# Zero warm-up, fewer first masks, a last fold in two parts and re-placed sums and loads in a fused attention, Fourier-mix and FFN kernel

## The chip, the cores and the metric

The kernel runs on 1 core of one Trainium2 chip. The metric is device time in microseconds (us) of one execution; lower is better. The engines are TensorE (PE, with its weight loads shown apart as PEld), VectorE (DVE), ScalarE (ACT), GpSimd (POOL) and SyncE (SP), which here issues nearly all DMAs.

## The reference

Windowed attention with sink tokens, then a block that adds a real 2-D Fourier transform, normalises, and runs a two-layer FFN. Shapes: 4 batches, 8 heads, 768 tokens, head size 64; so 512 channels, and a hidden size of 2048. All in float32; `n_sink` is 4 and `window` is 128.

```
scores = q @ k.T / sqrt(D)
keep   = (key < n_sink) | (0 <= query - key < window)
a      = softmax(where(keep, scores, -1e9))            # + 1e-9 in the denominator
x      = (a @ v), heads side by side                   # [4, 768, 512]
u      = x + real(fft(fft(x, tokens), channels))
un     = (u - mean(u)) / sqrt(var(u) + 1e-6)           # per token
out    = u + relu(un @ w_ch1) @ w_ch2                  # w_ch1 [512, 2048], w_ch2 [2048, 512], float64
```

## The kernel before

**Tiling.** Tokens are handled in 24 blocks of 128 (6 per batch, batches in the order 0, 2, 1, 3). One step of the attention loop (`window_attention`, L719) handles one pair of heads of one block, so 4 steps per block, 96 in all, numbered s. Every engine has an order of operations written out by hand for each of the four steps (`SCHEDULE`, L83), with delays against the step at which the scores were made (`STEP_LAG`, `BLOCK_AT`). Work beside the attention is hung into those steps by `at(step, engine, function)` and run by `run_ev`.

**The first steps.** The masks depend on `n_sink` and `window`, which a small DMA brings (`prm`, L242). VectorE builds mask 0 before step 0, all other masks but the last in `other_masks` (L971) in step 1, and `last_mask` (L985) in step 3. `mask[i]` is used by block i of a batch (block 3 and later use `mask[3]`), and `older[0]`, `older[1]` choose in `merge` (L788) between two key blocks. In step 3 also the sink values of batch 0 are split into a high and a low half (`SINK0_AT`, L763 to L769). TensorE meanwhile runs transposes of the identity that nobody reads (`warm_up`, L958): 11 before step 0 and 8, 0, 8, 4, 8, 4, 0 in steps 0 to 6.

**The Fourier part** of a batch (`fourier`, L336) begins when its blocks are there: `fold_n` (sums and differences of two token blocks), `fold_m` (the same along the channels), `fold_hi` and `fold_lo` (a float32r high half `gh` by ScalarE and a low half `gl` by VectorE), `stage1` (matmuls along the tokens; kinds a0, a1, r, b0, b1 by channel range), `stage2a/b` (along the channels), `combine` and `update` (add to the token block `u`). For the last batch (`tail`) the three folds all run on VectorE. Up to step 97 the program order is the order on each engine; from there to group 1 of the FFN a scheduler orders the instructions by readiness, with the program order as priority. `tc.issue_after(x)` holds an instruction behind x in that ordering.

**The FFN** works on 6 groups of 4 token blocks. Group 0 (the loop at L1343) goes through the 16 blocks f of the hidden size: `ch1` (12 matmuls of 512 columns, L703), `split` (relu and its high half on ScalarE, low half on VectorE, L1191), and one block behind it `ch2` (12 matmuls, L1199). In the same loop the float64 weights are turned into float32 pairs (`convert`, L627: three integer operations on VectorE, a copy on ScalarE, a subtraction on GpSimd: L651 for the first layer, L666 for the second). `combine_w1` (L671) forms sums of weight blocks on GpSimd (`tq`, four operations of 128x256, then two of 128x512 in `halves`, L686) and stores them to DRAM (`w_dram`), because groups 1 to 5 use a seven-product scheme (Strassen's, in Winograd's form) whose weights are such sums. Group 1's token side (`prepare_1`, L1261: statistics, normalising, transposing, then seven steps of token sums `sums_x`, L1284) also lies in this loop, three steps per block from f = 6 on.

**Group 1** (from L1405, again in hand-written order) streams its weight sums back: `load(n)` (L1390) issues two DMAs of 256 KB on SP into place n modulo 8; seven of the eight places are filled before group 1 starts, after all stores of `w_dram`. `product` (L1414) does 12 matmuls of 256 columns and issues the load for eight products later. `hring` (four slots, in the memory of `un_slots`, that is of `unT0`, which `ch1` of group 0 reads) takes the hidden values of group 1. `todo` (L1503) places group 2's statistics, normalising and transposes among group 1's steps; 10 steps make one of its four rounds `it`. Groups 2 to 5 have the same structure among themselves and are not touched, except by the places that `load` uses.

## Time and profile before

| | us |
|---|---|
| median of 3 runs | 746.86 (746.4 to 748.05) |
| the profiled execution's own time | 747.63 |
| its span (first to last instruction) | 745.9 |
| TensorE busy in the span | 715.6 (96%) |
| VectorE, ScalarE, GpSimd busy | 560.5 (75%), 357.3 (48%), 274.4 (37%) |

The time of the run contains 1.7 us that lie outside the span. Busy times of TensorE contain modelled ends, so a busy TensorE can still be held up a little; an idle one certainly is. The share over the whole span says little about this change, which touches the first 20 us, and the stretch from about 200 to 350 us. There the views by stretch and the lists in order of time have to be read.

### The profile page before, as it was taken

How to read it: one execution, taken by the hardware profiler on the slowest of the kernel's cores; microseconds unless marked ns; L12 is line 12 of the kernel's file. 1: busy time of each engine (PE TensorE's matmuls, PEld its weight loads, DVE VectorE, ACT ScalarE, POOL GpSimd, SP SyncE). 2: the span in 40 equal slices, each digit the busy share in tenths (PEclk: the TensorE clock that was granted, in tenths of full speed). 3: DMA queues.
4: the chain of work that ended last, by engine and by line, in shares of the span. 5: the costliest groups of instructions: out<-in, count | busy, mean ns of one | idle time of the engine just before them, and what ended most of it. 6: DMA issues, size and time to landing. Idle time of an engine off the chain costs nothing.

```text
span 745.9 us, 15695 instructions
## 1 busy us (share of the span) xinstructions
PE 715.6 (96%) x5539; PEld 642.6 (86%) x5539; DVE 560.5 (75%) x1299; ACT 357.3 (48%) x901; POOL 274.4 (37%) x391
## 2 busy tenths in 40 slices
PE   8999998989979999898999999999999999999996
PEld 6776876867868888687989999999999999999996
DVE  7778578888899988858668667947697578846773
ACT  5887666766634537313324134534444245523541
POOL 3567467577557989824994000000000000000000
PEclk9999999999999999999999999999999999999998
DMA  9863525533207999779999798979974897759721
GB/s 304 289 173 106 149 73 165 174 94 103 86 21 237 328 346 330 277 277 385 374 301 327 246 348 277 313 239 379 375 242 167 321 378 261 255 205 390 269 98 62
DMA packets 109576, 181.69 MB, mean 244 GB/s; under 512 B 9868, under 2 KB 44812, under 8 KB 108336
## 3 DMA queue, kind: packets, MB, share of 16 engines
q1 hardware_dynamic: 109200, 176.83, 69.6%
q0 software_dynamic: 288, 3.76, 1.3%
q8 instruction: 46, 0.75, 0.4%
q14 instruction: 42, 0.34, 0.1%
HBM read 148.04 MB, written 32.51 MB: 242 GB/s over the span
## 4 chain that ended last, share of the span: by engine, by line
PE 50%; DVE 4%; ACT 1%; issue 1%; SPq 0%; DMA 0%; POOL 0%; DVEq 0%
PE pB L1421 10%; PE qB L1598 9%; PE pA L1421 7%; PE pC L1421 6%; PE qC L1598 6%; PE qA L1598 6%; PE o L1449 5%; DVE bn L530 1%; PE unt L571 1%; DVE hring L1193 0%; DVE x L1657 0%; DVE x L1660 0%; SPq L1394 0%; DVE un L565 0%; DVE stat L531 0%
## 5 line engine op out<-in xcount | busy, mean ns | idle before, releaser
L1620 ACT CAST hring<-x 128x512 fp32r<-128x512 f32 x92 | 57.0, 619 | 52.0 <-PE qB L1598 19.6
L811 ACT ACTIVATE sm<-sm,mx 128x132 f32<-128x132 f32 x192 | 75.9, 400 | 4.6 <-DVE mx L805 4.6
L1624 DVE TENSOR_TENSOR hring<-x,hring 128x512 fp32r<-128x512 f32 x92 | 63.4, 689 | 14.8 <-ACT hring L1620 9.3
L786 PE MATMUL s<-ring,q 64*128 64x260 f32 x320 | 49.0, 411 | 5.9 <-DVE mx L805 2.7
L805 DVE CUSTOM_DVE_ANT_0 sm<-s,mask 128x132 f32<-128x132 f32 x192 | 48.5, 293 | 6.2 <-DVE s L792 0.9
L703 PE MATMUL h<-un_slots,w_ring 128*128 128x512 f32 x192 | 49.7, 405 | 3.4 <-POOL w_ring L651 2.9
L703 PEld LDWEIGHTS h<-un_slots,w_ring 128*128 128x128 f32 x192 | 36.3, 194 | 12.4 <-POOL w_ring L651 4.1
L786 PEld LDWEIGHTS s<-ring,q 64*128 64x128 f32 x320 | 26.9, 185 | 18.2 <-issue 5.0
L1598 PE MATMUL qA<-w,hring 128*128 128x256 f32 x312 | 39.8, 279 | 0.0
L1449 PE MATMUL o<-w,hring 128*128 128x512 f32 x156 | 38.5, 393 | 1.3 <-ACT hring L1192 1.1
L850 ACT COPY pta<-pt 128x512 f32<-128x512 f32 x48 | 28.1, 585 | 24.1 <-PE pt L843 24.0
L881 PE MATMUL xt<-ptl,ldv 128*64 128x128 f32 x384 | 39.3, 285 | 0.0
L1199 PE MATMUL o<-w,h_sb 128*128 128x512 f32 x156 | 38.1, 392 | 0.0
L1598 PEld LDWEIGHTS qA<-w,hring 128*128 128x128 f32 x312 | 37.9, 189 | 0.0
L811 ACT ACTIVATION_READ_ACCUMULATOR sm<-sm,mx 128x1 f32 x192 | 36.7, 191 | 0.0
L792 DVE COPY_PREDICATED s<-older,s 128x256 f32<-128x256 uint8 x80 | 33.7, 421 | 3.1 <-PE s L786 3.1
L859 POOL TENSOR_SCALAR_AFFINE_SELECT ptl<-pta 128x512 f32<-128x512 f32 x48 | 31.5, 655 | 11.6 <-ACT pta L850 11.6
L1598 PE MATMUL qB<-w_c,hring 128*128 128x256 f32 x288 | 35.2, 281 | 0.0
L1449 PEld LDWEIGHTS o<-w,hring 128*128 128x128 f32 x156 | 28.5, 188 | 7.5 <-ACT hring L1192 1.3
L881 PEld LDWEIGHTS xt<-ptl,ldv 128*64 128x64 f32 x384 | 22.1, 136 | 14.6 <-issue 4.8
L1598 PEld LDWEIGHTS qB<-w_c,hring 128*128 128x128 f32 x288 | 34.5, 189 | 0.0
L1199 PEld LDWEIGHTS o<-w,h_sb 128*128 128x128 f32 x156 | 29.1, 188 | 6.1
(296 smaller groups left out, 1965.3 us busy)
## 6 DMA issues: line engine op xcount, KB each, us to landing
w_c<-wd SPq DMA_DIRECT2D x96, 256.0 KB, 5.0
w_h<-wd SPq DMA_DIRECT2D x76, 256.0 KB, 5.1
w_t<-wd SPq DMA_DIRECT2D x70, 256.0 KB, 4.7
raw<-in_moe_w_ch_dram SPq DMA_DIRECT2D x32, 512.0 KB, 4.5
w_c<-td SPq DMA_DIRECT2D x48, 256.0 KB, 4.6
w_q<-wd SPq DMA_DIRECT2D x38, 256.0 KB, 5.0
wd<-to SPq DMA_DIRECT2D x8, 1024.0 KB, 6.4
ldv<-in_v_dram SPq DMA_DIRECT2D x28, 256.0 KB, 3.3
```

Of the source, the lines that this page charges most:

```text
L703: T.matmul(ps[:, :tb], a[cc], x[:, :, cc, :], start=n == 0, stop=n == 3 * NCC - 1)
L786: T.matmul(ps[:, j, :P + W], st["q", g][rows, hp, :], keys(g, 2 * hp + j), start=True, stop=True)
L792: V.copy_predicated(ps[:, :, P + NS:P + W], older[qi > 2], ps[:, :, 0:P])
L805: V.tensor_tensor_reduce(sm[:, h % 4], ps[:, j, P:P + W], mask[min(qi, 3)], -SCALE, 3.0e38, ALU.add, ALU.min, accum_out=mx[:, 0, h:h + 1])
L811: A.activation(sm[:, h % 4], sm[:, h % 4], AF.Exp, bias=mx[:, 0, h:h + 1], scale=-1.0, accum_out=mx[:, 1, h:h + 1])
L881: T.matmul(ps[D * j:D * j + D, p, :], st["v", kb(g) - i][:, h, :], a[:, h % 4, :], start=i == 0, stop=i == n - 1)
L1199: T.matmul(po[i], a[:, P * i:P * i + P], x, start=f == 0 and n == 0, stop=f == NF - 1 and n == 2)
L1421: T.matmul(ps[:, 256 * j:256 * j + 256], w[:, j, a, cs], x[:, xs], start=BANK.index(BANK[k]) == k and j == c == m == 0, stop=j == c == 1 a ...
L1449: T.matmul(po[i], h[:, a, j, ts_], x, start=first and j == m == 0, stop=last and j == 1 and m == 2)
L1598: T.matmul(ps[:, 256 * t:256 * t + 256], h[:, a, j, P * t:P * t + P], x, start=BANK.index(BANK[k]) == k and c == t == j == m == 0, stop=c ...
L1620: A.copy(hi, x)
L1624: V.tensor_tensor(*args, op=ALU.subtract)
```

## The change

Constants, the masks, the last fold, one fused subtraction on GpSimd, and the places of several steps:

- **Warm-up.** VectorE clears 96 columns of a scratch tile; TensorE runs 5 matmuls of 96x96 on those zeros, then 8 transposes in place of 11; step 0 has 5 in place of 8.
- **Masks.** Step 1 builds `older[0]` and `mask[1]` only; `mask[2]` is copied from them in step 5, `older[1]` and `mask[3]` come in step 8. The first sink split moves from step 3 to steps 5 and 6.
- **Folds of the last batch.** Blocks 0 and 1 fold 2 to 4 steps sooner after they are ready; block 2 is folded in two parts (channels 0 to 256, then 257 to 511), each through all four operations, the parts one step apart.
- **Places.** `ch1` of f = 1 moves from step 107 to 111, the updates of the third batch by two steps (`UPD_LATE`), the conversion of the second layer's first two blocks behind the split of f = 0.
- **Weight sums.** Two 128x256 subtractions of `combine_w1` become one of 128x512 (`q[:, 1:3]`), and are held behind the low half (L651) of the block's own second weight.
- **Group 1's token work.** The steps of `prepare_1` are spread (3, 3, 2, 2, 2, 1 in f = 6 to 11, none in 12, then the seven sum steps as 2, 2, 3 in f = 13 to 15), and each is held behind that block's relu and low half.
- **Loads.** The first four weight sums of group 1 go into the four slots of `hring`, issued once `ch1` of f = 15 is done with that memory, then three more, then the last stores of `w_dram`, then the rest. There are so twelve places at first and eight in turn after that.
- **Group 2's preparation** moves later in group 1: statistics from steps 0 to 2 to steps 3 to 7, the normalising from 5, 7, 9, 12 to 11, 12, 14, 22, the transposes from 7, 9, 12, 14 to 12, 14, 22, 24, with the two PSUM banks exchanged.

```diff
-UPD_LATE = 36
+UPD_LATE = 38
-CONV_AT, CH1_AT = (3, 5), (9, 10)
+CONV_AT, CH1_AT = (3, 5), (9, 14)
-PREP_N = 3
+PREP_N = {6: 3, 7: 3, 8: 2, 9: 2, 10: 2, 11: 1, 13: 2, 14: 2, 15: 3}
-WARM = 11
-WARM_STEP = (8, 0, 8, 4, 8, 4, 0)
+COLD, WARM = 5, 8
+WARM_STEP = (5, 0, 8, 4, 8, 4, 0)
-F_LAST = (1, 1), (2, 2), (3, 3)
+F_TAIL = (1, 1), (2, 2), (3, 3)
-SINK0_AT = 3, 3, "V"
+SINK0_AT = 5, 6, "V"
...
-                    f_n, f_m, f_s = F_LAST if tail and j == NHALF - 1 else (F_N, F_M, F_S)
+                    if tail and j == NHALF - 1:
+                        for i, cs in enumerate((slice(0, 257), slice(257, DM))):
+                            at(k + 1 + i, "V", lambda i=i, j=j: fold_n(V, j, i))
+                            at(k + 1 + i, "V", lambda i=i, j=j: fold_m(V, j, i))
+                            at(k + 2 + i, "A", lambda j=j, cs=cs: fold_hi(j, cs))
+                            at(k + 2 + i, 0, lambda j=j, cs=cs: fold_lo(j, cs))
+                        continue
+                    f_n, f_m, f_s = F_TAIL if tail else (F_N, F_M, F_S)
...
-                G.tensor_tensor(q[:, 1], b12, b11, op=ALU.subtract)
+                with tc.issue_after(state["lo", 2 * p + 1]) if p else ExitStack():
+                    G.tensor_tensor(q[:, 1:3], t[:, 1].rearrange("p (h c) -> p h c", h=2), t[:, :, :256], op=ALU.subtract)
                 G.tensor_tensor(q[:, 0], b22, q[:, 1], op=ALU.subtract)
-                G.tensor_tensor(q[:, 2], b22, b12, op=ALU.subtract)
...
+                        cold = take(96)
+                        V.memset(cold, 0.0)
...
+                        for i in range(COLD):
+                            T.matmul(warm[:96, i % 4, :96], cold, cold, start=True, stop=True)
                         warm_up(WARM, warm)
...
-                        at(1, "V", other_masks)
-                        at(3, "V", last_mask)
+                        at(1, "V", second_mask)
+                        at(5, "V", third_mask)
+                        at(8, "V", last_mask)
...
+            def place(n):
+                return hring[:, n] if n < NH else places[(n - NH) % NWS]
...
             for f in range(NF):
                 ps = hp.pop(0) if f < 2 else ch1(0, f, unT0)
+                if f == NF - 1:
+                    hring = npool.tile([P, 4, 2, 2, 256], F32R, tag="un_slots", name="hring", bufs=1)
+                    for n in range(NH):
+                        load(n)
...
                 split(hs[f], ps)
+                for i in (2, 3) if f == 0 else ():
+                    convert(i, wa)
...
-                for _ in range(PREP_N if f >= PREP else 0):
-                    next(steps, None)
+                for _ in range(PREP_N.get(f, 0)):
+                    with tc.issue_after(state["h_lo"]), tc.issue_after(state["relu"]):
+                        next(steps, None)
...
-                todo = {0: [(statistics, 0)], 1: [(statistics, 1, 2)], 2: [(statistics, 3)], 3: [(deviate, 7)], 5: [(deviate,), (make, 0)],
-                        7: [(turn, 0, *banks[1][:2]), (make, 1)], 9: [(turn, 1, *banks[1][:2]), (make, 2)],
-                        12: [(turn, 2, *banks[0][:2]), (make, 3)], 14: [(turn, 3, *banks[0][:2])]}
+                todo = {3: [(statistics, 0)], 4: [(statistics, 1)], 6: [(statistics, 2)], 7: [(statistics, 3)], 8: [(deviate, 1)],
+                        9: [(deviate, 1)], 10: [(deviate,)], 11: [(make, 0)],
+                        12: [(turn, 0, *banks[0][:2]), (make, 1)], 14: [(turn, 1, *banks[0][:2]), (make, 2)],
+                        22: [(turn, 2, *banks[1][:2]), (make, 3)], 24: [(turn, 3, *banks[1][:2])]}
```

More of the change, by code (lines that the diff above doesn't have):

```diff
@@ L1337, in do, with load @@
                     s += 1
+            T_PLACE = {1: 0, 2: 1, 4: 2, 6: 3}
+            stream = [(w_dram, it, W_PLACE[k]) for it in range(NIT) for k in range(7)]
+            for g in range(2, len(groups)):
+                stream += [(w_dram, i, W_PLACE[k]) for it in range(0, NIT, 2) for k in range(7) for i in (it, it + 1)]
+                stream += [(t_dram, it, T_PLACE[k]) for k in (1, 2, 4) for it in range(NIT)]
+            NH = 4
+            def place(n):
+                return hring[:, n] if n < NH else places[(n - NH) % NWS]
+            def load(n):
+                if n < len(stream):
+                    d, it, k = stream[n]
+                    for j in range(2):
+                        state["load"] = nc.sync.dma_start(f32(place(n)[:, j]).rearrange("p s c -> p (s c)"), d[2 * it + j][:, k]).ins
             po = [ps_o.tile([P, DM], F32, tag=f"o{i}", name=f"o{i}_0") for i in range(len(groups[0]))]
             hs = {}
-            for i in (2, 3):
-                convert(i, wa)
             for f in range(NF):
                 ps = hp.pop(0) if f < 2 else ch1(0, f, unT0)
+                if f == NF - 1:
+                    hring = npool.tile([P, 4, 2, 2, 256], F32R, tag="un_slots", name="hring", bufs=1)
+                    for n in range(NH):
+                        load(n)
                 hs[f] = g0.tile([P, 2, 512], F32R, tag="h", name=f"h_sb{f}", bufs=2)
@@ L1375, in run @@
                 late.pop()()
+            places = [npool.tile([P, 2, 2, 256], F32R, tag="ld", name=f"w1_c{i}", bufs=LDB) for i in range(LDB)]
+            with tc.issue_after(state["load"]):
+                for n in range(NH, NH + LDB):
+                    load(n)
             for i in sorted(stores):
-                for fn in stores.pop(i):
-                    fn()
-            places = [npool.tile([P, 2, 2, 256], F32R, tag="ld", name=f"w1_c{i}", bufs=LDB) for i in range(LDB)]
-            T_PLACE = {1: 0, 2: 1, 4: 2, 6: 3}
-            stream = [(w_dram, it, W_PLACE[k]) for it in range(NIT) for k in range(7)]
-            for g in range(2, len(groups)):
-                stream += [(w_dram, i, W_PLACE[k]) for it in range(0, NIT, 2) for k in range(7) for i in (it, it + 1)]
-                stream += [(t_dram, it, T_PLACE[k]) for k in (1, 2, 4) for it in range(NIT)]
-            def load(n):
-                if n < len(stream):
-                    d, it, k = stream[n]
-                    for j in range(2):
-                        nc.sync.dma_start(f32(places[n % NWS][:, j]).rearrange("p s c -> p (s c)"), d[2 * it + j][:, k])
+                with tc.issue_after(state["load"]) if i > 2 * NF else ExitStack():
+                    for fn in stores.pop(i):
+                        fn()
             w1_t = g0.tile([P, 2, 2, 2, 256], F32R, tag="to", name="w1_t")
-            places += [w1_t[:, 0], w1_t[:, 1], g0.tile([P, 2, 2, 256], F32R, tag="tq", name="w1_q")]
+            places += [g0.tile([P, 2, 2, 256], F32R, tag="tq", name="w1_q"), w1_t[:, 0], w1_t[:, 1]]
             places.append(g0.tile([P, 2, 2, 256], F32R, tag="h", name="w1_h0", bufs=2))
-            for n in range(NWS - 1):
-                load(n)
+            with tc.issue_after(state["load"]):
+                for n in range(NH + LDB, NH + NWS - 1):
+                    load(n)
             ch2(NF - 1, hs.pop(NF - 1), po)
@@ L1408, in run @@
                 places.append(g0.tile([P, 2, 2, 256], F32R, tag="h", name="w1_h1", bufs=2))
-                hring = npool.tile([P, 4, 2, 2, 256], F32R, tag="un_slots", name="hring", bufs=1)
                 more = [wr.tile([P, 2, 512], F32, name="more")] if general else []
@@ L1414, in product @@
                 def product(n, k, ps):
-                    w = places[n % NWS]
+                    w = place(n)
                     xh, xl = (t[:, k] for t in state["x"])
@@ L1593, in product2 @@
                             if k in (1, 2, 4):
-                                w = [places[n % NWS][:, j, a] for a in range(2)]
+                                w = [place(n)[:, j, a] for a in range(2)]
                             else:
```

40 lines of the change are left out of this document (22 added, 18 removed).

## Prediction

> **What bounds the kernel now.** I read the table of busy times by stretch first, because the change touches only the first 20 us and the stretch from the last attention blocks to group 1 of the FFN. Columns: the stretch, its length, busy time (and count) of PE, PEld, DVE, ACT, POOL, then TensorE's granted clock, DMA share and GB/s.
>
> ```profile
> 0.00:20.00 20.00, 16.77 (x120) 12.72 (x120) 13.99 (x79) 11.20 (x43) 6.64 (x24) 1.00 0.96 305
> 20.00:200.00 180.00, 170.99 (x1538) 132.62 (x1534) 141.93 (x574) 126.76 (x476) 114.22 (x225) 1.00 0.46 140
> 200.00:214.70 14.70, 14.46 (x118) 12.35 (x118) 14.60 (x25) 5.81 (x13) 9.19 (x11) 1.00 0.15 53
> 214.70:218.40 3.70, 2.33 (x15) 1.82 (x13) 3.70 (x7) 0.62 (x3) 3.62 (x5) 1.00 0.00 0
> 218.40:221.80 3.40, 1.23 (x4) 0.59 (x4) 3.40 (x7) 1.04 (x3) 0.37 (x1) 1.00 0.00 0
> 221.80:225.20 3.40, 3.36 (x9) 2.63 (x10) 3.40 (x7) 1.11 (x2) 1.51 (x2) 0.55 0.44 154
> 225.20:230.20 5.00, 5.00 (x27) 4.74 (x26) 4.30 (x8) 2.82 (x6) 3.59 (x4) 0.96 0.95 304
> 230.20:316.50 86.30, 83.44 (x396) 68.93 (x395) 78.70 (x129) 42.54 (x77) 76.93 (x75) 1.00 0.86 308
> 316.50:326.40 9.90, 9.90 (x44) 8.09 (x44) 3.58 (x6) 2.75 (x5) 5.77 (x6) 1.00 0.59 215
> 326.40:349.00 22.60, 19.06 (x131) 16.93 (x131) 17.23 (x34) 5.57 (x11) 3.27 (x4) 1.00 1.02 361
> 349.00:746.00 397.00, 389.07 (x3152) 381.22 (x3152) 275.72 (x433) 157.06 (x268) 49.25 (x44) 0.99 0.80 279
> ```
>
> TensorE is the bound nearly everywhere: 170.99 of 180 us to 200, 389.07 of 397 after 349. What can be won lies in four places. In the first 20 us it idles 3.2. From 214.7 to 221.8 (the last fold) it works 3.56 of 7.1 us while VectorE works all the time. Right behind that its clock is granted at 0.55. From 230.2 to 316.5 (group 0) it idles 2.9, with VectorE at 78.70 and GpSimd at 76.93 of 86.30: three engines near their limit together. From 326.4 to 349 (start of group 1) it idles 3.5. Groups 2 to 5 lie in the last row and aren't changed.
>
> **The first steps.** From the list in order of time (start, duration, engine, line; in brackets the idle time before and its end):
>
> ```profile
> 3.43 0.17 DVE L249 CAST pf<-prm 128x4 f32<-128x4 int32 x1 [1.34 <-DMA prm<-in_limits_dram]
> 5.89 1.44 PEld L960 LDWEIGHTS warm<-ident 128*128 128x128 f32 x8 [0.24 <-issue]
> 6.45 0.49 DVE L973 TENSOR_SCALAR older<-scratch 128x256 uint8<-128x256 f32 x2
> 7.39 0.23 DVE L979 COPY mask<-nosink 128x4 f32<-128x4 f32 x2
> 7.86 0.48 DVE L983 TENSOR_SCALAR mask<-scratch,eff 128x128 f32<-128x128 f32 x2
> 8.14 1.29 PEld L960 LDWEIGHTS warm<-ident 128*128 128x128 f32 x12
> 13.34 0.43 DVE L792 COPY_PREDICATED s<-older,s 128x256 f32<-128x256 uint8 x1 [0.72 <-PE s L786]
> ```
>
> Nothing before step 0 can gain: VectorE starts its masks when the limits land (3.43), whatever TensorE does. The five zero matmuls have no row; eight transposes took 1.44 us of weight loads early and twelve took 1.29 later (0.18 and 0.11 each), so five cost 0.5 to 0.9 us, in a time in which TensorE first sat idle to 1.8 us; three transposes fewer pay them back. The clear on VectorE lies in its wait for the first index tile. Step 1 loses half of 0.49, all of 0.23 and half of 0.48: 0.72 us of VectorE. TensorE loses three of eight transposes in step 0: 0.54. The next scores and their reductions come so 0.5 to 0.7 sooner. What is left out there comes back in steps 5, 6 and 8, on the same engine, which had 6.0 us idle in the first 20, among them the 0.72 at 13.34. Nothing else is queued on VectorE there that a matmul needs sooner than a step later. Against it, DMA is at 0.96 in this stretch, so a key block could land at its own time and cap the gain. I take 0.7 us, bounds 0 and 1.5; from 20 us on TensorE is busy enough to keep the lead.
>
> **The last fold.**
>
> ```profile
> 208.20 1.27 DVE L355 TENSOR_TENSOR f<-us,us 128x512 f32<-128x512 f32 x2
> 216.07 0.95 PE L446 MATMUL b<-cst,zb 128*128 128x258 f32 x6 [1.05 <-DVE d L452]
> 218.20 0.86 DVE L462 TENSOR_TENSOR u<-u,d 128x257 f32<-128x257 f32 x1
> 218.98 0.62 PE L398 MATMUL za<-cst,gh 128*128 128x386 f32 x2 [0.91 <-ACT gh L368]
> 219.91 0.68 DVE L371 TENSOR_TENSOR gl<-f,gh 128x512 fp32r<-128x512 f32 x1
> 220.64 0.44 PE L398 MATMUL za<-cst,gl 128*128 128x386 f32 x1 [1.04 <-DVE gl L371]
> 221.84 3.53 PE L703 MATMUL h<-un_slots,w_ring 128*128 128x512 f32 x8 [0.59 <-DVE h_sb L1193]
> ```
>
> TensorE waits 1.05 + 0.91 + 1.04 + 0.59 = 3.6 us, each time for VectorE. Its queue there holds block 1's fold, conversions, an update (0.86) and then block 2's low half at 219.91. The change folds blocks 0 and 1 sooner, puts conversions 2 and 3 behind the split and the update two steps on. A part of block 2 needs a sum (0.64, half of 1.27), the channel fold and a half-width low part (about 0.4 each, as 0.68 for the whole), so the first part is done 1.5 us after the block is stored and the second 1.5 later; splitting adds some 0.2 us of VectorE. The kinds a0 and a1 (channels 0 to 255) need only the first. I leave 1.0 us of the 3.6, since the first wait is for another operation (L452) that stays behind VectorE's queue: 2.6 won. Moving `ch1` of f = 1 behind these matmuls costs nothing as long as its own input, the free PSUM bank after the low half of f = 0, was late anyway: that was the 0.59.
>
> The clock: 0.55 over 3.4 us and 0.96 over 5.0 cost 1.5 + 0.2 = 1.7 us of TensorE. The drop stands right behind the two stretches in which TensorE worked 2.33 of 3.70 and 1.23 of 3.40; no single wait was over 1.05 us. With 2.6 us less idle time the second would look like the first, behind which the clock held. I take the 1.7, with 0 as the other bound. [...]
>
> **Group 0.** From the grouped list of GpSimd from 222 to 326 (busy, mean ns | idle before), the list in order of time, and VectorE's waits there (total, times, longest):
>
> ```profile
> L651 POOL TENSOR_TENSOR w_ring<-tw,w_ring 128x512 fp32r<-128x512 f32 x14 | 18.8, 1342 | 0.0
> L679 POOL TENSOR_TENSOR tq<-tw 128x256 f32<-128x256 f32 x7 | 6.4, 914 | 0.0
> L677 POOL TENSOR_TENSOR tq<-tw 128x256 f32<-128x256 f32 x7 | 5.7, 815 | 4.7 <-DVE tw L641 3.6 <-DVE stat L542 1.0
> 301.20 1.06 POOL L677 TENSOR_TENSOR tq<-tw 128x256 f32<-128x256 f32 x1 [2.48 <-DVE tw L641]
> 305.95 2.56 PE L703 MATMUL h<-un_slots,w_ring 128*128 128x512 f32 x10 [1.36 <-POOL w_ring L651]
> 313.23 2.56 PE L703 MATMUL h<-un_slots,w_ring 128*128 128x512 f32 x10 [1.49 <-POOL w_ring L651]
> DVE h_sb L1193 <- ACT h_sb L1192: 7.1, 4, 2.7
> ```
>
> TensorE stalls 1.36 and 1.49 for the low half of a first-layer weight (L651). At 301.20 GpSimd ran the sums `tq` first and L651 after them; the new hold turns that round, which covers the 1.36. One 128x512 operation (1.34, by L651) for two (0.82 + 0.91) saves 0.4 us per weight pair, 2.8 in seven. GpSimd also waited 2.48 for VectorE at 301.20, when VectorE was in the token sums that now come from f = 13 on. Together that covers the 2.85. But TensorE now arrives 4.3 us sooner (2.6 + 1.7), and needs weights sooner: GpSimd has 86.30 - 76.93 = 9.4 us idle plus the 2.8, VectorE 7.6, to move up by 7. That is enough in sum, not in every block. I give back 1.6: 2.6 + 1.7 + 2.85 - 1.6 = 5.5 us by the end of group 0; bounds 1.5 (the tail's 4.3 lost to weights, half the stalls kept) and 8.2 (all of 3.6, 1.7 and 2.85).
>
> **Group 1.**
>
> ```profile
> 323.88 0.32 SPq L687 DMA_DIRECT2D wd<-to  x1
> 324.30 2.97 SPq L1394 DMA_DIRECT2D w_c<-wd  x4
> 329.55 1.69 PE L1421 MATMUL pB<-x,w_c 128*128 128x256 f32 x12 [1.30 <-DMA w_c<-wd]
> 335.82 0.21 ACT L540 ACTIVATE stat<-stat 128x4 f32<-128x4 f32 x1 [2.44 <-DVE stat L537]
> 336.57 0.72 PE L1449 MATMUL o<-w,hring 128*128 128x512 f32 x2 [1.07 <-ACT hring L1192]
> 348.85 1.68 PE L1421 MATMUL pB<-x,w_c 128*128 128x256 f32 x12 [0.96 <-ACT xf L1257]
> w_c<-wd SPq DMA_DIRECT2D x96, 256.0 KB, 5.0
> ```
>
> Three waits make 3.3 us. The second product waited for its weights, queued on SP behind the store of the last sums (323.88). Now eight loads go out when `ch1` of f = 15 is done (about 5 us before group 1), ahead of that store. At 0.74 us per issue (2.97 for four) and 5.0 to landing, place 0 is there 5.7 us after that, each next place 1.5 later, while products take 1.4 to 1.6: 0.5 us of waiting at most. The stores behind them are read back far later. The relu at 336 stood on ScalarE behind a square root that waited for VectorE's statistics; those move behind it. The wait at 348.85 was for a PSUM bank that a transpose held; the banks are exchanged. The moved statistics have 22.60 - 17.23 = 5.4 us of idle VectorE there and more behind. Taking 3.5 of idle less 0.5: 3.0 us, bounds 0.5 and 3.5.
>
> **The sum.** 0.7 + 5.5 + 3.0 = 9.2 us. The profiled execution took 747.63 (1.7 outside its span of 745.9), so 738.4; the median stands 0.77 below it: 737.7.
>
> **The rivals.** First: the weights keep their times. In group 0 GpSimd and VectorE are so full (76.93 and 78.70 of 86.30) that an earlier TensorE only waits more for L651. Then 1.5 of 5.5 stay, and with a group 1 of 2.0 and the 0.7 the gain is 4.2: 742.7. For it speak the two waits for L651 at the end of the stage, against it the freed 2.8 us and GpSimd's 9.4 idle. Second, slower: in nine blocks the token work is held behind the low half L1193, and everything behind that on VectorE, conversions too, waits for TensorE's `ch1` and the relu. Such waits took 7.1 us in four places, 1.8 each, 2.7 at most. With 2.7 in all nine it is 24.3, of which 7.6 is idle time VectorE has; 16.7 less the gains elsewhere (0.7 + 4.3 + 3.0 = 8.0) gives 8.7 slower, 755.6. It decides from 1.8 us per block. Against it: what is held was there to fill gaps. Third: the change doesn't do what it says, because the ordering by readiness leaves folds and sums about where they were; with the 0.7 and half a microsecond of loads the time is 745.7.
>
> **How the numbers follow.** The forecast 0.66, weights late 0.20, no effect 0.05, slower 0.09. The range of 8 in 10 goes from 733.0 (all upper bounds, 13.2 us of gain, make 733.7) to 744.0, past the first rival; outside lie the other two and a rest. About 0.2% (1.5 us) is what a measurement can tell from no change: faster 0.86, same 0.05, slower 0.09.
>
> **What would show it.** Right: no stretch around 215 to 228 with a granted clock under 1, TensorE waits there of about 1 us in sum; no wait for L651 over 1 us, and `tq` behind L651; the second product of group 1 without a DMA wait over 0.5; the rows from 349 on unchanged in length. Wrong: the same idle sum in group 0 under other names (L651, L1193), a clock still at half, or products of group 1 waiting for token sums that came too late.

## The result and the profile after

The kernel after takes 755.44 us (median of 6 runs, 753.76 to 757.54), the kernel before, on the same chip, 747.1 (6 runs): a ratio of 1.011, 95% interval 1.0088 to 1.0132. It is slower by 8 us where the prediction had it 9 us faster, and outside the range. The profiled execution of after took 755.78 us, its span 754.1.

The same stretches as before, cut at the same places of the work (length, busy time and count of PE, PEld, DVE, ACT, POOL, granted clock, DMA share, GB/s):

```profile
0.00:20.00 20.00, 16.34 (x107) 12.38 (x107) 13.85 (x78) 9.39 (x35) 6.12 (x21) 0.91 0.96 321
20.00:200.00 180.00, 170.94 (x1515) 131.93 (x1515) 137.15 (x563) 124.68 (x473) 112.58 (x221) 0.98 0.46 136
200.00:219.10 19.10, 18.40 (x156) 15.68 (x154) 18.67 (x33) 9.65 (x26) 12.02 (x16) 1.00 0.17 56
219.10:230.30 11.20, 9.79 (x53) 8.75 (x53) 11.09 (x22) 5.22 (x12) 5.76 (x6) 1.00 0.25 60
230.30:316.80 86.50, 84.74 (x395) 70.20 (x395) 77.86 (x128) 39.52 (x72) 73.22 (x65) 0.98 0.88 312
316.80:329.20 12.40, 10.76 (x46) 7.90 (x45) 10.66 (x14) 6.15 (x11) 10.68 (x8) 1.00 0.69 245
329.20:357.20 28.00, 23.20 (x146) 21.09 (x144) 19.95 (x35) 5.82 (x11) 6.62 (x8) 0.94 0.96 343
357.20:754.00 396.80, 387.97 (x3136) 380.65 (x3136) 274.56 (x434) 156.67 (x267) 44.87 (x41) 0.99 0.80 276
```

Read the clock column first. Before, the only dip ahead of the very end was behind the last fold; that one is gone (1.00 from 200 to 230). In its place stand four others: 16.4 to 26.7, 282.7 to 286.1, 337.3 to 340.7 and 357.8 to 361.2 us. The fold and what follows it took 3.70 + 3.40 + 3.40 + 5.00 = 15.5 us before and take 11.2 here (219.1 to 230.3): it began 4.4 us later and ends level.

Where the time went shows best when a fixed point of the work is followed through both traces. The table gives the start of a TensorE instruction, kernel minus kernel before, in us of the profiled executions (negative is earlier); the other columns are experiments below.

| point of the work | after | sink back | fold alone | three undone | three undone, later normalising |
|---|---|---|---|---|---|
| `ch1(0)` | +4.36 | -0.79 | -0.13 | -0.65 | -0.15 |
| `ch1(2)` | +0.13 | -5.03 | -4.37 | -4.87 | -4.38 |
| `ch1(8)` | +0.13 | -5.03 | -4.38 | -4.87 | -4.38 |
| `ch1(10)` | +3.88 | -2.88 | -3.03 | -2.43 | -3.76 |
| `ch1(15)` | +0.33 | -6.31 | -0.86 | -5.98 | -5.68 |
| end of group 0's `ch2` | +2.74 | -3.89 | -0.90 | -3.58 | -3.21 |
| group 1, product 1 | +1.29 | -5.35 | +1.63 | -5.05 | -4.67 |
| product 7 | +3.38 | -2.72 | +2.86 | -5.09 | -4.76 |
| product 14 | +6.53 | +1.94 | +2.85 | -5.00 | -4.75 |
| first of group 2 (product 28) | +7.51 | +2.92 | +2.85 | -4.49 | -4.25 |
| end of the span | +8.16 | +3.79 | +2.45 | -3.52 | -3.52 |

So in after the start loses 4.4, the fold wins 4.2, group 0 loses 2.6, group 1 loses 4.8, and the rest 0.6. The profiled execution of before (747.63) was 0.5 to 0.8 us above that kernel's medians, so the columns flatter by about that.

**The start.** Four rows of before, then four of after, from the lists in order of time:

```profile
8.89 0.62 ACT L765 CAST vs<-vt 128x512 fp32r<-128x512 f32 x1 [2.28 <-DMA vt<-in_v_sink_dram]
11.79 0.78 POOL L298 DMA_DIRECT2D cst<-in_dft_dram  x1
14.35 0.98 SPq L748 DMA_DIRECT2D ring<-in_qk_dram  x1
15.38 5.40 SPq L755 DMA_DIRECT2D ldv<-in_v_dram  x2
```

```profile
8.77 0.78 POOL L298 DMA_DIRECT2D cst<-in_dft_dram  x1
13.38 0.69 DVE L777 TENSOR_TENSOR vs<-vt,vs 64x512 fp32r<-64x512 f32 x1 [1.71 <-ACT vs L773]
13.57 5.26 SPq L756 DMA_DIRECT2D ring<-in_qk_dram  x1
15.29 0.71 PE L794 MATMUL s<-ring,q 64*128 64x260 f32 x4 [1.76 <-issue]
```

Two things changed that the prediction did not cost, both from moving the sink's split from step 3 to 5 and 6. The low part on VectorE now waits 1.71 us for its high part, which stands on ScalarE behind the exponentials of step 5; while VectorE waits it merges no scores, and TensorE, which needs the banks of merged scores, idles 1.76 us (that one follows from the other is for the runs to show). And ScalarE, no longer held 2.28 us for the sink's DMA in step 3, lets GpSimd come 3 us sooner to its request for the Fourier constants (3.3 MB); SP's next request for keys is then stuck for 5.26 us in place of 0.98. In before a stall of that length stands too, but on the two requests behind it, for values (5.40 us for both).

**Group 0.** Three rows of after:

```profile
282.16 0.66 PE L578 MATMUL unt<-ident,un 128*128 128x128 f32 x4 [1.57 <-ACT un L570]
324.19 3.24 PE L1217 MATMUL o<-w,h_sb 128*128 128x512 f32 x12 [0.69 <-POOL w L673]
328.38 1.21 PE L1217 MATMUL o<-w,h_sb 128*128 128x512 f32 x4 [0.95 <-POOL w L673]
```

The waits of 1.36 and 1.49 for w_ring's low half are gone, as predicted. In their place TensorE waits for the normalised tile of group 1, whose transposes stand too early in its queue, and for the low half of second-layer weights.

**Group 1.** Three rows of after at its start, four from its second round:

```profile
329.70 0.32 SPq L661 DMA_DIRECT2D wd<-w_ring  x1
336.18 0.59 ACT L1566 COPY tmp<-pA 128x512 f32<-128x512 f32 x1 [9.89 <-DMA wd<-w_ring]
336.82 2.57 PE L1452 MATMUL pA<-x,hring 128*128 128x256 f32 x12 [3.00 <-ACT tmp L1566]
...
353.71 2.52 POOL L1514 TENSOR_TENSOR tmp<-tmp 128x512 fp32r<-128x512 f32 x2 [3.85 <-ACT tmp L1513]
353.81 1.22 DVE L555 SCALAR_TENSOR_TENSOR stat<-stat 128x4 f32<-128x4 f32 x1
355.06 1.20 DVE L557 TENSOR_TENSOR stat<-stat 128x4 f32<-128x4 f32 x1
358.15 1.09 PE L578 MATMUL unt<-ident,un 128*128 128x128 f32 x4 [2.75 <-DVE un L572]
```

The second product has its weights. But the last store of `w_ring`, now behind the loads, is issued at 329.70 and not at 316.55. `tmp` takes over w_ring's memory, so the copy of the first product waits 9.89 us for that store, and the fourth product, which needs the first one's bank, 3.00. Later the transposes of group 2's tokens (moved to step 12) wait 2.75 us for statistics that are late as well.

### The profile page after: what moved, and what is told of

Read it like the earlier page. It is cut to its first block, busy times and chain, and to the rows that moved or that the text cites. A ratio compares the mean times of both kernels' runs of the same rounds, so it can differ in the third digit from the quotient of the medians.

```text
span 754.1 us, 15689 instructions
## 1 busy us (share of the span) xinstructions
PE 722.1 (96%) x5543; PEld 648.6 (86%) x5543; DVE 563.8 (75%) x1301; ACT 357.1 (47%) x902; POOL 271.9 (36%) x383
## 3 DMA queue, kind: packets, MB, share of 16 engines
q0 software_dynamic: 288, 3.76, 1.2%
## 4 chain that ended last, share of the span: by engine, by line
PE 71%; DVE 13%; POOL 5%; ACT 4%; issue 3%; DMA 3%; SPq 1%; ACTq 0%; DVEq 0%; POOLq 0%
PE pB L1452 9%; PE qB L1631 9%; PE pA L1452 7%; PE pC L1452 6%; PE qA L1631 6%; PE qC L1631 6%; PE o L1481 5%; PE xt L889 4%; PE s L794 4%; PE h L711 3%; PE o L1217 2%; PE pt L851 2%; PE za L397 2%; PE unt L578 1%; DVE bn L537 1%
## 5 line engine op out<-in xcount | busy, mean ns | idle before, releaser
L794 PE MATMUL s<-ring,q 64*128 64x260 f32 x320 | 51.0, 427 | 7.4 <-DVE mx L813 2.6
L1452 PE MATMUL pB<-x,w_c 128*128 128x256 f32 x348 | 45.2, 283 | 0.0
L1452 PEld LDWEIGHTS pB<-x,w_c 128*128 128x128 f32 x348 | 43.2, 191 | 0.0
L889 PEld LDWEIGHTS xt<-ptl,ldv 128*64 128x64 f32 x384 | 22.4, 140 | 15.4 <-issue 4.3
```

Of the source, the lines that this page charges most:

```text
L794: T.matmul(ps[:, j, :P + W], st["q", g][rows, hp, :], keys(g, 2 * hp + j), start=True, stop=True)
L889: T.matmul(ps[D * j:D * j + D, p, :], st["v", kb(g) - i][:, h, :], a[:, h % 4, :], start=i == 0, stop=i == n - 1)
L1452: T.matmul(ps[:, 256 * j:256 * j + 256], w[:, j, a, cs], x[:, xs], start=BANK.index(BANK[k]) == k and j == c == m == 0, stop=j == c == 1 a ...
```

## The experiments

Each is compared with the kernel before, run on the same chip: 747.0 to 747.2 us, in the second set 746.6. Waits in the expectations are partly excess from start to start, some 0.15 us above the idle times of the rows.

**Sink back.** Kernel after, with

```diff
-SINK0_AT = 5, 6, "V"
+SINK0_AT = 3, 3, "V"
```

> The kernel after, with the first sink's high and low parts back in step 3. Theory A (order of the transfers): in the kernel before, ScalarE and with it GpSimd waited in step 3 for the sink values, and so the GpSimd queue asked for the large constants at 11.79 us; in the kernel after it asks at 8.77 us, ahead of the third query block's packets, which land at 15.53 instead of 13.32 us; TensorE then idles 2 us at 13.3 us and its clock is at half from 16.4 to 26.7 us. With the sink back the constants are asked for near 11.8 us again, the query block lands near 13.3 us, no half clock stands before 27 us, and the time falls by 4 to 5 us, to about 751. Rival B (the shorter warm-up itself, five products of zeros in place of real transposes, leaves the clock without credit): the half clock at 16 to 27 us stays, and the time stays within 1 us of 755.4.

Measured: 751.68 us, ratio 1.0061 (1.0046 to 1.0076). The constants are asked for at 11.60, no half clock before 27 us, `ch1(0)` 0.79 sooner than in before. The whole loss at the start comes from this one line; without it the start gains 0.79 here, close to the 0.7 of the prediction. This kernel then lost 4.7 us from product 7 to 14, with a half clock at 351 to 358 us; that is the transposes' wait, not the start.

**Constants later.** Kernel after, sink left late:

```diff
-                                        if (s, op) == (4, "G"):
+                                        if (s, op) == (6, "G"):
```

> The kernel after, with the sink's parts left in steps 5 and 6, and the constants asked for by GpSimd in step 6 instead of step 4. By theory A it is the time of this request and not the place of the sink's parts that matters: the request then comes 1 to 2 us later, the third query block lands between 13.3 and 15.5 us, TensorE's idle time at 13 us falls below 1 us, the half clock before 27 us is gone, and the time falls by 4 to 5 us. If it is rather the sink's parts that now fall into the steps of the second block and hold ScalarE (rival C), the idle time of TensorE at 13 us and the half clock stay, and the time is within 1 us of 755.4.

Measured: 751.75 us, ratio 1.0072 (1.0052 to 1.0092). Here theory A was half wrong:

```profile
13.17 0.69 DVE L777 TENSOR_TENSOR vs<-vt,vs 64x512 fp32r<-64x512 f32 x1 [1.72 <-ACT vs L773]
13.36 0.63 SPq L756 DMA_DIRECT2D ring<-in_qk_dram  x1
15.03 0.78 POOL L298 DMA_DIRECT2D cst<-in_dft_dram  x1
15.08 2.18 PE L794 MATMUL s<-ring,q 64*128 64x260 f32 x8 [1.76 <-issue]
```

The constants come at 15.03, 6 us later than in after, and TensorE's 1.76 us of idle time is still there to the digit, with VectorE's 1.72 ahead of it: in this it was rival C, the sink's own parts, and not the third query block. (That VectorE's wait for the high part is the link is read from the rows; no run moves the low part alone.) What went is SP's stall (0.63) and two of the three periods of half clock (15.4 to 18.8 remains). By `ch1(0)` 3.6 of the 4.4 us are back.

**Sink late in the kernel before.** There,

```diff
-SINK0_AT = 3, 3, "V"
+SINK0_AT = 5, 6, "V"
```

> The kernel before, with nothing changed but the sink's parts moved from step 3 to steps 5 and 6. Theory A: the constants are asked for 3 us earlier, the third query block lands 2 us later, TensorE idles 2 us at about 13 us, the clock is at half for some 10 us behind it, and the kernel before becomes 3 to 5 us slower (about 751). Rival B (it takes the new warm-up on zeros): this edit alone costs under 1 us, and no half clock stands before 27 us.

Measured: 750.61 us, ratio 1.0038 (1.0016 to 1.006). `ch1(0)` starts 3.65 us later; half clock from 18 to 25 us. The edit costs this by itself, without the new warm-up (from sink back to after it is 5.15).

**Filling the wait.** Kernel after, with `WARM_STEP = (5, 0, 8, 4, 8, 4, 0, 24)`.

> The kernel after, with 24 more warm-up transposes put on TensorE in step 7, into the time in which it waits for the third query block; the block lands as late as before. This tells the wait from the clock behind it: if the loss at the start is mostly the half clock, and that follows from TensorE's idle time between 13 and 16 us, then TensorE stays busy through that time, the clock stays full, and the time falls by 3 to 4 us (to about 752) though the scores of the third block still start near 15.3 us. If the clock falls for another reason than the idle time (power of the work itself, a fixed time after the start), the half clock stays and the time is the same or up to 1 us longer.

Measured: 753.6 us, ratio 1.0097 (1.0076 to 1.0118); `ch1(0)` at +4.76. A miss that tells something:

```profile
13.22 2.78 PE L971 MATMUL warm<-ident 128*128 128x128 f32 x24
13.42 7.31 SPq L756 DMA_DIRECT2D ring<-in_qk_dram  x1
25.10 2.10 PE L794 MATMUL s<-ring,q 64*128 64x260 f32 x8 [3.64 <-DMA ring<-in_qk_dram]
```

The clock stayed full up to 24.8 us. But TensorE then waited 3.64 us for keys whose request SP had been stuck with for 7.31 us, and the fourth token block's scores began at 25.10, against 24.52 in after, where that row has no wait. A full clock alone won nothing. In the six traces with the constants asked for at 8.7 to 8.8 us (after, this one, sink late in the kernel before, and three of those below: ring store first, old places, no hold), `ch1(0)` comes 3.0 to 4.8 us late, with one to three periods of half clock before it; with the request at 15.03 it is 0.80, with one. The start's loss is thus mostly the transfers' order, and the sink's own parts are the smaller share. What the half clock adds to it is not told apart.

**Ring store first.** Kernel after, with

```diff
                     hring = npool.tile([P, 4, 2, 2, 256], F32R, tag="un_slots", name="hring", bufs=1)
+                    for i in (2 * NF, 2 * NF + 2):
+                        for fn in stores.pop(i, ()):
+                            fn()
                     for n in range(NH):
                         load(n)
```

> The kernel after, with the last store of w_ring (and the store of the seventh pair's sums) issued ahead of the first four weight loads into hring, as it stood ahead of them in the kernel before; the last store of the sums stays behind. Theory D (the store moved behind the loads): w_ring's store is then issued before 322 us instead of at 329.70, lands before 327 instead of at 336.08, the first copy into tmp does not wait 9.89 us for it, the idle time of 3.00 us on TensorE before the third bank's product and the half clock at 337 to 341 us go, and the time falls by 3 to 5 us (to about 751), part of it if the half clock then falls elsewhere. Rival E (the first products' weights, not the buffer, are late): the loads into hring then come 1 us later, the wait moves to them, and the time is within 1 us of 755.4.

Measured: 750.49 us, ratio 1.0048 (1.003 to 1.0066).

```profile
318.50 0.33 SPq L661 DMA_DIRECT2D wd<-w_ring  x1
330.74 0.59 ACT L1569 COPY tmp<-pA 128x512 f32<-128x512 f32 x1 [4.76 <-issue]
333.32 1.57 PE L1455 MATMUL pA<-x,hring 128*128 128x256 f32 x12
```

Theory D holds: no wait at the copy or at the fourth product, no half clock there, and product 5 starts 4.9 us sooner than in after. The loads into hring cost nothing by starting after the store.

**Old places of group 2's preparation.** Kernel after, with the `todo` of before (its first and last entries here):

```diff
-                todo = {3: [(statistics, 0)], 4: [(statistics, 1)], 6: [(statistics, 2)], 7: [(statistics, 3)], 8: [(deviate, 1)],
+                todo = {0: [(statistics, 0)], 1: [(statistics, 1, 2)], 2: [(statistics, 3)], 3: [(deviate, 7)], 5: [(deviate,), (make, 0)],
...
-                        22: [(turn, 2, *banks[1][:2]), (make, 3)], 24: [(turn, 3, *banks[1][:2])]}
+                        12: [(turn, 2, *banks[0][:2]), (make, 3)], 14: [(turn, 3, *banks[0][:2])]}
```

> The kernel after, with the steps of the third group's normalisation in the places of the kernel before (statistics in steps 0 to 2, deviations in 3 and 5, transposes in 7, 9, 12, 14). Theory F (the late places collide): the transposes of the second set of products wait no more for the normalised tile, so the 2.75 us of TensorE at 358 us and the half clock at 358 to 361 us (1.7 us) go, the stretch from product 7 to product 14 falls from 26.14 towards the 22.99 us of before, and the time falls by 3 to 4 us. The 3.00 us at 336 us stays. Rival G (the early places cost as much, now that the first products come without waits): a wait of 2 us or more on the transposes in steps 7 and 9, and the time within 1 us of 755.4.

Measured: 753.74 us, ratio 1.0103 (1.0064 to 1.0142). Product 7 to 14 takes 23.0 us, as in before, not 26.14, so theory F holds there. The total fell by less than expected: in this run the wait at the copy (3.27 us here) was followed by twice the time at half clock, 336 to 343 us. The statistics' operations were short:

```profile
341.92 0.17 DVE L555 SCALAR_TENSOR_TENSOR stat<-stat 128x4 f32<-128x4 f32 x1
342.12 0.17 DVE L557 TENSOR_TENSOR stat<-stat 128x4 f32<-128x4 f32 x1
```

**No hold.** Kernel after, with group 1's token steps not held behind the relu:

```diff
-                    with tc.issue_after(state["h_lo"]), tc.issue_after(state["relu"]):
-                        next(steps, None)
+                    next(steps, None)
```

> The kernel after, with the steps of the second group's normalisation no longer held behind the high and low parts of the block's relu; their numbers per block stay. Theory H (the hold delays the normalised tiles for the transposes in TensorE's queue): the wait of 1.57 us and the others before the transposes at 275 to 290 us go, with the half clock at 283 to 286 us, and ch1(8) to ch1(10) takes 12 us as in the kernel before (11.94) instead of 15.69; the time falls by 2 to 4 us. Rival I (what costs there is the number of steps put into blocks 6 to 10 and the engines' contention): the stretch still takes 14 us or more, and the relu's low part comes later, so that second products wait; the time is the same or 1 to 3 us longer.

Measured: 757.35 us, ratio 1.0148 (1.0126 to 1.017), slower than after. The stretch from `ch1(8)` to `ch1(10)` took 13.67 us, between the two expectations, without the wait of 1.57 and without a half clock; at blocks 12 and 14 the waits for w_ring's low half were back (1.26 and 1.01). Taken together group 0 got shorter without the hold: from `ch1(8)` to its end it lost 1.39 us against before, and 2.61 in after. The loss lies behind it:

```profile
336.43 0.59 ACT L1565 COPY tmp<-pA 128x512 f32<-128x512 f32 x1 [12.62 <-DMA wd<-w_ring]
337.07 2.93 PE L1451 MATMUL pA<-x,hring 128*128 128x256 f32 x12 [5.75 <-ACT tmp L1565]
```

TensorE came sooner to the copy that waits for w_ring's store, and the store came no sooner: 5.75 us of waiting in place of 3.00, and twice the time at half clock behind it (334.7 to 341.6). So the slower total does not show that the hold pays; in group 0 of this kernel it cost 1.2 us, the half clock at 283 us included.

**The fold alone**, in the kernel before, with all that belongs to it:

```diff
-UPD_LATE = 36
+UPD_LATE = 38
-CONV_AT, CH1_AT = (3, 5), (9, 10)
+CONV_AT, CH1_AT = (3, 5), (9, 14)
...
+                    if tail and j == NHALF - 1:
+                        for i, cs in enumerate((slice(0, 257), slice(257, DM))):
...
+                for i in (2, 3) if f == 0 else ():
+                    convert(i, wa)
```

> The kernel before, with the two-part fold of the last token block alone (its steps, the later update and second first-product, and the third and fourth conversion behind the first relu). The prediction had 2.6 us of idle time and 1.7 us of half clock go at 210 to 235 us; in the kernel after 4.2 us went there. Expected: ch1(2) starts 4 to 5 us earlier than in the kernel before, no half clock at 222 to 226 us, nothing else changed by over 0.5 us, and the time falls by 4 to 5 us, to about 742.5. Rival: half of the gain needs the other parts (the earlier start, the placed normalisation steps): 2 us or less.

Measured: 750.62 us, ratio 1.0055 (1.0037 to 1.0073): slower than before, though the fold does all it should (-4.37 at `ch1(2)`, no half clock there). What follows eats it:

```profile
275.67 1.19 PE L1205 MATMUL o<-w,h_sb 128*128 128x512 f32 x4 [0.98 <-POOL w L672]
298.01 4.11 PE L709 MATMUL h<-un_slots,w_ring 128*128 128x512 f32 x10 [1.42 <-POOL w_ring L657]
313.97 2.56 PE L709 MATMUL h<-un_slots,w_ring 128*128 128x512 f32 x10 [1.46 <-POOL w_ring L657]
331.18 2.93 PE L1427 MATMUL pB<-x,w_c 128*128 128x256 f32 x12 [3.83 <-DMA w_c<-wd]
```

TensorE comes sooner to weights that come no sooner: the wait for group 1's first weights grew from 1.30 to 3.83 us, and half clock followed twice (298.7 to 302.1, 329.4 to 336.2). This is the prediction's first rival, stronger than priced.

**Three undone.** Kernel after, with sink back, ring store first, and the old `todo`.

> The kernel after with three edits undone together: the sink back in step 3, w_ring's last store ahead of the loads into hring, the third group's normalisation in its old steps. If the three losses are separate and add: 4.4 us (the sink alone), 3.9 us (the store alone) and 3.1 us (the stretch from product 7 to 14 alone, 26.14 to 22.99), so 755.4 - 11.4 = 744 us, 3 us below the kernel before. Rival (the later stages are tied to data that come no earlier: the weights' way through conversion, GpSimd and the stores): most of the third gain and part of the second are eaten by waits for the weights or by further half clocks, and the time is 747 to 750.

Measured: 745.4 us, ratio 0.9982 (0.9969 to 0.9996): 10.0 of the 11.4 us, and a little below before. No half clock is left ahead of the end.

**The old normalising too.** The last kernel without the hold, and

```diff
-PREP_N = {6: 3, 7: 3, 8: 2, 9: 2, 10: 2, 11: 1, 13: 2, 14: 2, 15: 3}
+PREP_N = {f: 3 for f in range(6, 16)}
```

> The kernel before this one in the list, with the second group's normalisation also as in the kernel before: three steps a block from block 6 on, none held behind the relu. If the spread-out numbers and the holds cost what the trace of after shows (ch1(8) to ch1(10) 15.69 us instead of 11.94, of it 1.7 of half clock): the stretch is back near 12 us, and the time 2 to 4 us below that of the kernel with three edits undone (to about 741). Rival (the spread was what removed the waits of 1.53 and 1.66 us for w_ring's low parts in the kernel before): these waits come back at blocks 12 and 13, and the time is within 1 us of that kernel.

Measured: 749.91 us, ratio 1.0028 (1.001 to 1.0046). Its trace also shows a half clock at 105 to 109 us, where nothing was changed. Counted from `ch1(8)` to the end of group 0 it is 2 us longer than the last kernel: the waits for w_ring came back (1.04 and 0.90 at block 12, 1.68 at block 14), as its rival had it. The time did not follow the rival: it is 4.5 us above that kernel and not within 1.

**The sums' order on GpSimd alone**, in the kernel before:

```diff
-                G.tensor_tensor(q[:, 1], b12, b11, op=ALU.subtract)
+                with tc.issue_after(state["lo", 2 * p + 1]) if p else ExitStack():
+                    G.tensor_tensor(q[:, 1:3], t[:, 1].rearrange("p (h c) -> p h c", h=2), t[:, :, :256], op=ALU.subtract)
                 G.tensor_tensor(q[:, 0], b22, q[:, 1], op=ALU.subtract)
-                G.tensor_tensor(q[:, 2], b22, b12, op=ALU.subtract)
```

> The kernel before, with the sums of the first weights alone as in after: two subtractions on GpSimd in one instruction, and issued behind the low part of the pair's second block. Theory (it is the order on GpSimd that made first products wait for w_ring's low part): the two waits of 1.53 and 1.66 us at 304 and 311 us go and the last second product ends 3 us earlier, and the time falls by 2 to 3 us if the first products of the second group have their weights by then. Rival (rate, not order: the weights come no faster through loads, conversion and stores): the waits move to the second product's low parts or to the DMA of w_c, which waits 1.47 us already, and the time is within 1 us of 747.

Measured: 753.35 us, ratio 1.009 (1.0063 to 1.0116); its profiled run was the shortest of five, 750.02, so the trace shows half the loss. In it the waits only move: 1.60 us for the normalised tile at 286 us, 1.16 and 2.18 for w_ring at 302 and 316. Where the other 3 us went stays open.

**Early weights alone**, in the kernel before, the ring's store kept first; the change's order of loads, and in block 15

```diff
+                if f == NF - 1:
+                    hring = npool.tile([P, 4, 2, 2, 256], F32R, tag="un_slots", name="hring", bufs=1)
+                    for i in (2 * NF, 2 * NF + 2):
+                        for fn in stores.pop(i, ()):
+                            fn()
+                    for n in range(NH):
+                        load(n)
```

> The kernel before, with the second group's first four weights loaded early into hring, and w_ring's last store kept ahead of them. Prediction's term for this part: 3.0 us of waits among the first products go. Expected by it: product 1 starts 1.4 to 1.5 us earlier and products 4 to 7 keep it, the time falls by 1.5 to 3 us, to about 744.5. Rival (the other places are free no earlier, so the transfers queue behind each other): the wait reappears at products 4 to 8, for DMA, and the time is within 1 us of 747.

Measured: 749.22 us, ratio 1.0031 (1.0015 to 1.0048). Product 1 comes 1.5 us sooner against the end of group 0, as expected; 2.5 us are lost again from product 21 to 28, and 1.6 after that, for reasons that stay open. This trace shows something else. Its last fold is that of the kernel before, with the same four waits of 1.05, 0.91, 1.04 and 0.59 us, and yet there is no half clock (the two stretches that had 1.23 us busy at clock 1.00 and 3.36 at 0.55 in before):

```profile
218.40:221.80 3.40, 1.27 (x5) 0.64 (x5) 3.40 (x7) 1.04 (x3) 0.28 (x1) 1.00 0.00 0
221.80:225.20 3.40, 3.40 (x16) 2.89 (x17) 3.40 (x8) 1.41 (x3) 1.62 (x2) 1.00 0.60 159
```

From `ch1(0)` to `ch1(2)` it takes 24.41 us, before 25.17, and the kernels with the new fold 20.9. So with the same waits the half clock at the fold came in the one execution and not in the other, and was worth 0.8 us by the start of `ch1(2)`.

**Normalising one block later.** Three undone, and

```diff
-PREP_N = {6: 3, 7: 3, 8: 2, 9: 2, 10: 2, 11: 1, 13: 2, 14: 2, 15: 3}
+PREP_N = {6: 4, 7: 1, 8: 1, 9: 2, 10: 2, 11: 2, 12: 1, 13: 2, 14: 2, 15: 3}
```

> The kernel with three edits undone (745.4 us), with the second group's normalisation spread otherwise: all four statistics in block 6, the deviations alone in block 7, the first make in block 8, the first transpose in block 9, so one block later each. If the wait of 2.05 us for the normalised tile (at 276.8 us there) comes from the transposes standing one block too early in TensorE's queue: it goes, ch1(9) to ch1(10) takes 6 to 6.5 us instead of 8.41, and the time falls by 1.5 to 2.5 us, to about 743.4. Rival (data-bound: what comes earlier waits at blocks 12 to 14 for GpSimd's low parts): the wait for w at blocks 13 and 14 grows from 1.97 us to 4 us and the time stays within 1 us of 745.4.

Measured: 744.2 us, ratio 0.9954 (0.9935 to 0.9973): below the kernel before and the lowest median here, though its interval still touches that of three undone. The row of three undone and the one that takes its place:

```profile
279.06 0.66 PE L578 MATMUL unt<-ident,un 128*128 128x128 f32 x4 [1.89 <-ACT un L570]
```

```profile
284.15 2.57 PE L711 MATMUL h<-un_slots,w_ring 128*128 128x512 f32 x10 [0.93 <-POOL w_ring L658]
```

`ch1(9)` to `ch1(10)` takes 6.42 us in place of 8.41, but 0.9 comes back as a wait for w_ring, and the end of group 0 gains nothing in the trace. The gain in the median (1.2 us) is below what was expected.

**The old order on GpSimd** in three undone: the diff of the sums' order above, the other way round.

> The kernel with three edits undone (745.4 us), with the sums of the first weights on GpSimd as in the kernel before (three subtractions in its order, none held behind the low part). If the new order is a gain of its own: the waits for w_ring's low part (1.5 and 1.7 us in the kernel before) come back at blocks 12 and 13, and the time rises by 1 to 3 us. Rival (the order only moves the wait from the first products to the second ones and to the normalised tile, as the kernel before with this edit alone suggests, which got 6 us slower): the time is within 1 us of 745.4 or lower by up to 3 us.

Measured: 745.21 us, ratio 0.9972 (0.9957 to 0.9986), as the rival had it: the same. The new order of the sums is worth nothing here. The 1.89 us for the normalised tile stay, so the order is not their cause in this kernel; the place of the transposes is, since the run with normalising one block later has none.

**Later normalising, no hold.** The kernel before this one but one, with the hold's diff from above.

> The kernel of the first run of this list (normalisation one block later), and its steps no longer held behind the relu's high and low parts. If the hold matters little once the steps stand late enough: within 1 us of that kernel. If the hold is what keeps the second products' parts in time (the kernel after without it lost 2 us): 1 to 3 us slower than it. If the hold itself delays the normalised tile: 1 to 2 us faster.

Measured: 747.83 us, ratio 1.0011 (0.9994 to 1.0028), 3.6 us slower than with the hold; block 14 then waits 2.54 us for w_ring, with a half clock behind it (312.4 to 315.8). Here the hold pays. That fits a hold that keeps VectorE and ScalarE free for conversions, which is argued, not shown.

## Why the prediction was wrong

Forecast were gains of 0.7 at the start, 4.3 at the fold, 1.25 in group 0 and 3.0 in group 1. The trace of after shows 4.4 lost, 4.2 won, 2.6 lost and 4.8 lost.

**The start (0.7 us): right for what it costed, wrong for what it left out.** With the sink back the table shows 0.79, 0.65 and 0.15 won (three kernels whose start was left alone differ from before by up to 0.3). The step that failed: "What is left out there comes back in steps 5, 6 and 8, on the same engine ... Nothing else is queued on VectorE there that a matmul needs sooner than a step later". The sink's low part, put on VectorE there by the same change, waits 1.71 us for ScalarE, and merges are queued behind it. And a wait that went (2.28 us on ScalarE) had set when GpSimd issued 3.3 MB. Together 4.4 us lost.

**The fold (2.6 + 1.7): the sum right, its parts in part by luck.** 4.2 us in after, 4.2 alone, and no half clock there in after (granted clock 1.00 from 215 to 228 us) nor, from 210 to 229 us, in three undone and the four kernels built on it; with the old fold, before and the sums' order alone have it (222.16 and 222.84 us), early weights alone has not. But by the early-weights trace, which has the old fold and no half clock, the waits and what hangs on them were worth 3.5 us and the half clock 0.8. One detail was misread: of the four waits put down to VectorE, the second (0.91) ended with ScalarE's copy, which itself waited for VectorE. The dip came in before with gaps of at most 1.05 us and is gone with the new fold; but the same gaps without a dip, in the early-weights trace, show that their length alone does not decide.

**Group 0 (2.85 less 1.6): its waits went, its sum did not.** With the clock full, three undone lost 1.3 us from `ch1(8)` to the end of group 0 where 1.25 were to be won. I counted idle GpSimd and VectorE time and gave back 1.6 ("enough in sum, not in every block"); the blocks decided. The idle time stayed under other names, a sign of being wrong that the prediction had named: in after 1.57 us for group 1's normalised tile and 0.69 and 0.95 for second-layer weights, in place of 1.36 and 1.49. The fold alone shows it too: 3.5 of its 4.4 us were gone by the end of group 0, a half clock among them. In after a half clock behind the wait for the normalised tile made it 2.6.

**Group 1 (3.0): the failed sentence is "The stores behind them are read back far later".** True of the data, but the store also reads w_ring, whose memory `tmp` needs with the first product: 3.9 us by the run with the store first (spans of 754.1 and 750.1). And for the moved statistics I counted 5.4 us of idle VectorE, which is room, and did not ask who waits for them: 3.1 us. Without both, product 1 keeps its 1.5 us, half of what was forecast.

**The rivals.** The slower one gave 755.6, and 755.44 was measured, but that is chance. Its mechanism, the hold behind the relu, was to cost 16.7 us in group 0; group 0 lost 2.6 in all, and 1.4 with the hold taken out. In the kernel with later normalising, taking the hold out made it 3.6 us slower. The first rival, weights that keep their times, is what happened to the fold's gain in the kernel before.

## What to carry to other kernels

When a step is moved later, ask what its wait was holding back: here a wait on one engine had set the time of a large transfer on another. When a store is moved behind loads, ask not only who reads it back but who needs its source's memory. And a part that gains by itself can lose in the whole: the earlier TensorE reached weights that came no sooner, so the pieces have to be tried together. For the same reason a kernel that gets slower when a part is taken out does not prove that the part pays: without the hold, group 0 was shorter, and what it won went into the wait for a store.

## What the runs showed of the hardware

The granted clock fell to half behind single waits of 1.57 and 2.75 us. Pairs of stretches of after, the one ahead of a dip and the dip:

```profile
279.30:282.70 3.40, 1.75 (x9) 1.22 (x10) 3.37 (x7) 1.99 (x4) 1.97 (x3) 1.00 1.00 417
282.70:286.10 3.40, 3.40 (x11) 2.62 (x10) 3.16 (x6) 2.74 (x5) 1.29 (x1) 0.50 0.43 86
...
354.40:357.80 3.40, 1.00 (x5) 0.50 (x3) 3.33 (x5) 0.17 (x1) 3.32 (x5) 1.00 1.01 300
357.80:361.20 3.40, 3.05 (x15) 3.08 (x16) 2.93 (x4) 1.62 (x3) 2.55 (x3) 0.50 1.03 353
```

The first stretch of each pair is the 3.4 us ahead of the dip. In the traces of before and after all changes of the clock lie whole multiples of 3.41 us apart (in after at 16.44, 26.68, 282.68, 286.09, 337.29, 340.70, 357.77, 361.18 and 750.30 us, in before at 222.16, 225.57 and 740.99). Cut into stretches of 3.41 us on from the first full clock that the traces record (6.20 us in after, 7.12 in before) to 735 us, TensorE was busy ahead of the drops for 1.42, 1.72, 0.47 and 1.04 us in after and for 1.55 in before; in every other stretch it was busy for at least 2.14 us in after and 1.92 in before. Other runs fill the space between: the clock fell behind 1.09 busy us in the old normalising too (102.07 to 105.48), 1.11 in later normalising, no hold (308.98 to 312.39) and 1.89 in the sums' order alone (219.43 to 222.84), and held behind 1.67 in three undone (275.50 to 278.91), 1.73 in the old normalising too (313.69 to 317.10) and 1.80 in the sums' order alone (284.28 to 287.69). So no one busy time parts the two.

The 1.27 of 3.40 busy us of the early-weights trace lie across a boundary of such stretches, with 2.03 and 2.25 us busy in the two, and the clock held. In before, with the same four waits, 1.55 lay in one of them, and it fell. That the place of the boundary makes the difference is inferred from these two traces. Ahead of the end, the dips of after lasted 10.24 us once and 3.41 three times, that of before 3.41, and one of the fold alone 6.8 (329.4 to 336.2). At the granted clock of 0.50, 3.41 us hold 1.7 us of full-clock work; by this estimate the wait of 1.57 us in after cost about twice its length. At the fold 0.8 of the 1.7 came through.

A VectorE operation on 128x4 took 1.22 us beside GpSimd's 128x512 subtractions (after, 353.81) and 0.17 without them (old places, 341.92). The reciprocal took 0.17 us inside a GpSimd operation too (after, 278.62). The addition of a constant on L544 took 1.14 us beside GpSimd (three undone, 273.19) and 0.16 with GpSimd idle (old places, 341.26). So two of these three small operations took some seven times as long beside GpSimd's work.
